# Two of the three output tiles of the second feed-forward layer by Strassen's seven products

## The chip, the core and the metric

The kernel runs on 1 core of one Trainium2 chip. The metric is the device time of one execution in microseconds (us), the median of 3 timed runs; a profile of one execution is read beside it.

## The reference

Attention with a decaying state over 4 batches, 8 heads, 768 positions of 48 values gives a matrix of 3072 tokens by 384. Two feed-forward layers follow, each 384 to 2048 to 384; the change lies in the second.

```python
x = attn_out.transpose(0, 2, 1, 3).reshape(B * S, H * D)     # 3072 x 384
h = x @ w_in;  x = (h - np.tanh(h)) @ w_out                  # layer 1
h = x @ w_in2
g = np.maximum(h, 0.0) + alpha * np.minimum(h, 0.0)          # alpha: one value per inner column
y = g @ w_out2                                               # layer 2
```

## The kernel before, in words

Every 32-bit factor of a layer's products is split into two fp32r tiles, a rounded high part (index 0) and the rest (index 1), and a product is the sum of three TensorE products: high by high, low by high, high by low (`terms`). Tokens are worked in 6 blocks j of 512 columns (`N2`), the inner 2048 columns in 16 tiles f of 128 (`KF`), the 384 columns of input and output in 3 tiles (`KC`).

One entry of `steps` is a layer, a block and an inner tile (l, j, f). A step issues, in this order of the code, which is also the order of every engine's queue:

- `mm_h` (L410): 9 products of 512 columns into one PSUM bank h; the banks 3 and 4 alternate.
- `elem_a` (L422): g from h. In layer 1 ScalarE (ACT) does the tanh, L426, and VectorE (DVE) the difference, L427. In layer 2 VectorE does both, `ga`, L429, and `gb`, L430.
- `elem_hi` (L434) on ScalarE and `elem_lo` (L438) on VectorE, issued in the next step, split gb into g, high part L436 and low part L441.
- `mm_acc1` or `mm_acc2` (L471) for the step two back (`LAG = 2`): 9 products of 512 columns, three for each of the 3 output tiles, each tile in a PSUM bank of its own. In layer 2 the blocks use the banks 0, 1, 2 and 5, 6, 7 in turn. After f = 15 each bank is copied out (L486, L484) and stored (L487).

Beside the products, in block 5 of layer 1 and block 0 of layer 2, the weights of layer 2 are turned from 64-bit words into fp32r parts by `conv_stage`: two checking passes (L108, L109), the low words (L81) and the high part (L100) on ScalarE, three operations (L94 to L96) on VectorE, the low part (L87) on GpSimd. Steps f = 6, 8 and 10 of each block of layer 2 but the last split the next block's input, `split_x2` (L495): a copy, L500, on ScalarE and a difference, L501, on GpSimd. In the attention, up to block 4 of layer 1, TensorE also has short 32-bit products: the scores `sc` (L260) and the transposes `kt` (L269). `keep_clock` and the `warm` argument of `mm_h` put idle bf16 products of 512 columns ahead of the first steps (L544, L415).

A flag computed from the inputs chooses between this program and a general one, `emit_general`, that the inputs here do not need.

Of the kernel before, what the change touches and what calls it, by code (L numbers as in the profile page):

```python
# [10 lines left out]
F32 = mybir.dt.float32  # L11
F32R = mybir.dt.float32r
# [17 lines left out]
N2 = 512  # L30
# [120 lines left out]
def emit_fast(nc, tc, qkav, w1, w2, alpha2, cst, out, x2d, c):  # L151
# [223 lines left out]
    def conv_stage(l, f, stage):  # L375
        if not 0 <= f < KF:
            return
        slot = f if l == 1 else f - EXT
        pool, tag = (wp, f"w{slot}") if slot >= 0 else (extp, f"e{f}")
        if stage == 0:  # L380
            raw_t[l, f] = conv[l].load(f, pool, tag)
        elif stage == 1:
            if l == 2:
                conv[l].check(raw_t[l, f][1], extp.tile([128, 2 * DM], BF16, tag="junk2", name="junk2"), f)
# [24 lines left out]

    terms = ((0, 0), (1, 0), (0, 1))  # L410

    def mm_h(l, f, x, n, bk, warm=0):
# [5 lines left out]
        for k, (a, b, ct) in enumerate(order):  # L418
            nc.tensor.matmul(h, w[:, a, ct * 128:(ct + 1) * 128], x[:, b, ct, :], start=(k == 0), stop=(k == 8))  # L419
# [12 lines left out]

    def elem_hi(s):
        gb, n = gb_of[s]  # L434
# [37 lines left out]
    def mm_acc2(j, f, g):  # L472
        if f == 0:
            banks = (0, 1, 2) if j % 2 == 0 else (5, 6, 7)
            acc[j] = [bank(b, [128, N2], f"o{c}") for c, b in enumerate(banks)]
        w = w_t[2, f]
        for c in range(KC):
            for i, (a, b) in enumerate(terms):
                nc.tensor.matmul(acc[j][c], w[:, a, DM + c * 128:DM + (c + 1) * 128], g[:, b, :],  # L479
                                 start=(f == 0 and i == 0), stop=(f == KF - 1 and i == 2))  # L480
            if f == KF - 1:
                e = extp.tile([128, N2], F32, tag="oe", name="oe", bufs=3)
# [4 lines left out]
                nc.sync.dma_start(out[c * 128:(c + 1) * 128, j * N2:(j + 1) * N2], e)  # L487

    x2f = {}

    def load_x2(j):
        t = extp.tile([128, KC, N2], F32, tag="x2f", name="x2f", bufs=2)
        nc.sync.dma_start(t, x2d[j])
        x2f[j] = t

# [234 lines left out]
    rechecks = {2 * KF + 4 + 2 * f: f for f in range(KF)}  # L730

    def mm_acc(s):
        l, j, f = steps[s]
        (mm_acc1 if l == 1 else mm_acc2)(j, f, g_of.pop(s))

    for s in range(F0, len(steps) + LAG):
        conv_1 = early.get(s, ())
        for f, stage in conv_1:
            if stage == 3:
                conv_stage(1, f, 3)  # L740
        if s - 1 in gb_of and s > F0:
            elem_hi(s - 1)
        if s < len(steps):
            l, j, f = steps[s]
            h = mm_h(l, f, x_t[j] if l == 1 else x_t["x2", j], N2, hb[s % 2])
            if s == u0:
                actx.close()
                extp = ctx.enter_context(tc.tile_pool(name="ext", bufs=1))
            for k, stage in conv_1:
                if stage != 3:  # L750
                    ops = conv_stage(1, k, stage)
                    if ops:
                        chains.append(ops)
            for k, stage in late.get(s, ()):
                conv_stage(2, k, stage)
            if s in rechecks:
                recheck(rechecks[s])
            if l == 1 and j == NB - 1:
# [18 lines left out]
            gb_of[s] = elem_a(l, f, h, N2), N2  # L777
            for piece in mid.get(s, ()):
                piece()
        elif s - 1 in gb_of:  # L780
            elem_lo(s - 1)
            run_chains()
        if s >= LAG + F0:
            mm_acc(s - LAG)
    ctx.close()


# [129 lines left out]
```

## Time and profile before

| what | value |
|---|---|
| median of 3 timed runs | 914.12 us (914.07 to 914.89) |
| profiled execution, its span | 913.0 us |
| TensorE busy | 899.1 us, 98% of the span |
| VectorE busy | 577.6 us, 63% |
| ScalarE busy | 367.7 us, 40% |
| GpSimd busy | 88.8 us, 10% |
| granted TensorE clock, all 40 slices | 9 tenths or more |

The span runs from the first to the last instruction of the profiled execution. Layer 2 begins near 514 us of it, its block 1 near 580 us, its last product ends near 906 us. A busy TensorE is one that always has a product in flight; how fast the products follow each other has to be read from the times of a row of equal ones. PE names TensorE's products, PEld its weight loads, DVE VectorE, ACT ScalarE, POOL GpSimd.

### The profile page before, as it was taken

What the parts mean: (1) busy time and instruction counts of PE and PEld (TensorE: products, weight loads), DVE (VectorE), ACT (ScalarE), POOL (GpSimd) and SP (SyncE); (2) the same over time, 40 slices, a digit from 0 to 9 for tenths busy, and PEclk for the clock granted to TensorE, in tenths of its full rate; (3) what the DMA queues carried; (4) which work ended last, traced back from release to release, by engine and by line L of the source; (5) the groups of instructions that cost most, each with busy time, mean ns of one, the idle gap of its engine ahead of it and who ended that gap; (6) DMA issues with size and microseconds to landing.
All of it is one profiled execution on the core that took longest, in us unless ns stands there. A gap on an engine that the chain in (4) does not pass through costs nothing.

```text
span 913.0 us, 13390 instructions
## 1 busy us (share of the span) xinstructions
PE 899.1 (98%) x5552; PEld 727.7 (80%) x5552; DVE 577.6 (63%) x835; ACT 367.7 (40%) x674; POOL 88.8 (10%) x82
## 2 busy tenths in 40 slices
PE   7899999999999999999999999999999999999997
PEld 4678887788888888788888888888888888888885
DVE  8998987766665565565466798555555555555553
ACT  2465555334545555543577665221221221221111
POOL 1110000100000000000034325010010010010000
PEclk9999999999999999999999999999999999999999
DMA  9575002124333334300364140200200100000001
GB/s 348 225 275 222 0 1 82 50 90 151 117 116 133 138 143 152 129 2 1 139 218 162 35 173 1 70 0 1 70 1 1 69 1 1 35 1 0 36 1 38
DMA packets 18212, 78.24 MB, mean 86 GB/s; under 512 B 2144, under 2 KB 2400, under 8 KB 15584
## 3 DMA queue, kind: packets, MB, share of 16 engines
q1 hardware_dynamic: 17856, 77.18, 23.0%
q8 instruction: 45, 0.74, 0.3%
q14 instruction: 23, 0.19, 0.1%
q10 hardware_dynamic: 288, 0.13, 0.1%
HBM read 67.87 MB, written 9.44 MB: 85 GB/s over the span
## 4 chain that ended last, share of the span: by engine, by line
PE 97%; DVE 2%; issue 0%; ACT 0%; POOL 0%; POOLq 0%
PE h L419 43%; PE acc L458 22%; PE o L479 21%; PE sc L260 3%; PE y L294 1%; PE idle L544 1%; PE y L307 1%; PE U L324 1%; PE y L298 1%; PE kt L269 1%; DVE iA L231 1%; DVE P L281 1%; PE y L302 0%; DVE A L220 0%; DVE x L339 0%
## 5 line engine op out<-in xcount | busy, mean ns | idle before, releaser
L419 PE MATMUL h<-x,w 128*128 128x512 f32 x1728 | 423.5, 390 | 0.6 <-ACT w L100 0.5
L419 PEld LDWEIGHTS h<-x,w 128*128 128x128 f32 x1728 | 324.4, 188 | 68.9 <-ACT w L100 1.0
L436 ACT CAST g<-gb 128x512 fp32r<-128x512 f32 x192 | 119.1, 620 | 349.0 <-DVE gb L430 272.5
L458 PE MATMUL acc<-g,w 128*128 128x512 f32 x864 | 216.5, 395 | 0.0
L479 PE MATMUL o<-g,w 128*128 128x512 f32 x864 | 211.2, 389 | 0.0
L441 DVE TENSOR_TENSOR g<-gb,g 128x512 fp32r<-128x512 f32 x192 | 135.8, 707 | 101.7 <-ACT g L436 101.5
L479 PEld LDWEIGHTS o<-g,w 128*128 128x128 f32 x864 | 162.2, 188 | 33.5
L458 PEld LDWEIGHTS acc<-g,w 128*128 128x128 f32 x864 | 159.5, 188 | 35.5 <-issue 0.8
L427 DVE TENSOR_TENSOR gb<-h,ga 128x512 f32<-128x512 f32 x96 | 66.1, 689 | 115.5 <-ACT ga L426 115.5
L429 DVE TENSOR_SCALAR ga<-h,al 128x512 f32<-128x512 f32 x96 | 72.0, 749 | 85.9 <-PE h L419 85.9
L426 ACT ACTIVATE ga<-h 128x512 f32<-128x512 f32 x96 | 56.5, 589 | 90.0 <-PE h L419 89.9
L430 DVE SCALAR_TENSOR_TENSOR gb<-h,ga 128x512 f32<-128x512 f32 x96 | 66.4, 691 | 3.3
L221 POOL TENSOR_TENSOR qkav_t<-qkav_t,A 128x512 f32<-128x512 f32 x20 | 24.6, 1232 | 367.0 <-DVE ac L222 324.8
L501 POOL TENSOR_TENSOR x<-x2f,x 128x512 fp32r<-128x512 f32 x18 | 24.4, 1355 | 237.0 <-ACT x L500 235.1
L87 POOL TENSOR_TENSOR w<-cv,w 128x384 fp32r<-128x384 f32 x32 | 35.5, 1128 | 103.9 <-DVE g L441 51.6
L100 ACT CAST w<-cv 128x768 fp32r<-128x768 f32 x32 | 26.7, 835 | 28.0 <-DVE cv L96 28.0
L231 DVE TENSOR_TENSOR_SCAN iA<-qkav_t,d1s 128x516 f32<-128x516 f32 x20 | 36.2, 1808 | 0.7
L95 DVE SCALAR_TENSOR_TENSOR cv<-raw,cv 128x768 uint32<-128x768 uint32 x32 | 35.2, 1101 | 0.1
L281 DVE TENSOR_TENSOR P<-sc,mask 128x512 f32<-128x512 f32 x48 | 30.8, 682 | 1.1 <-PE sc L260 0.7
L96 DVE CUSTOM_DVE_ANT_0 cv<-raw,cv 128x1536 uint16<-128x1536 uint16 x32 | 30.5, 952 | 0.6
L243 ACT ACTIVATE junk<-qkav_t,lim 128x512 bf16<-128x512 f32 x40 | 29.0, 724 | 0.7
L81 ACT ACTIVATE raw<-raw 128x768 uint32<-128x768 uint32 x32 | 28.9, 902 | 0.0
(84 smaller groups left out, 483.1 us busy)
## 6 DMA issues: line engine op xcount, KB each, us to landing
raw<-w SPq DMA_DIRECT2D x48, 768.0 KB, 6.4
qkav_t<-qkav SPq DMA_DIRECT2D x20, 1028.0 KB, 5.0
x2d<-x2e SPq DMA_DIRECT2D x18, 256.0 KB, 2.2
x2f<-x2d SPq DMA_DIRECT2D x6, 768.0 KB, 5.7
out<-oe SPq DMA_DIRECT2D x18, 256.0 KB, 2.1
qv<-qkav SPq DMA_DIRECT2D x8, 256.0 KB, 6.8
ak<-qkav SPq DMA_DIRECT2D x3, 516.0 KB, 7.0
ak<-qkav SPq DMA_DIRECT2D x1, 260.0 KB, 3.6
```

The lines of the kernel that those rows point to most:

```text
L87: self.nc.gpsimd.tensor_tensor(w[:, 1, i:i + DM], t.bitcast(F32)[:, i:i + DM], w[:, 0, i:i + DM].bitcast(F32), op=ALU.subtract)
L231: lambda: nc.vector.tensor_tensor_scan(iA[:, AW - 1:0:-1], a[:, AW - 1:0:-1], d1s[:, AW - 1:0:-1], 1.0, op0=ALU.mult, op1=ALU.add),
L281: nc.vector.tensor_tensor(P, scs[u], mask[:, None, :].to_broadcast([128, 4, CH]), op=ALU.mult)
L419: nc.tensor.matmul(h, w[:, a, ct * 128:(ct + 1) * 128], x[:, b, ct, :], start=(k == 0), stop=(k == 8))
L426: nc.scalar.activation(ga, h, ACTF.Tanh)
L427: nc.vector.tensor_tensor(gb, h, ga, op=ALU.subtract)
L429: nc.vector.tensor_scalar(ga, h, 0.0, al2[:, f:f + 1], op0=ALU.min, op1=ALU.mult)
L430: nc.vector.scalar_tensor_tensor(gb, h, 0.0, ga, op0=ALU.max, op1=ALU.add)
L436: nc.scalar.copy(g[:, 0], gb)
L441: chains.append([lambda: nc.vector.tensor_tensor(g[:, 1], gb, g[:, 0].bitcast(F32), op=ALU.subtract)])
L458: nc.tensor.matmul(acc[j][c], w[:, a, DM + c * 128:DM + (c + 1) * 128], g[:, b, :], start=(first and i == 0), stop=(last and i == 2))
L479: nc.tensor.matmul(acc[j][c], w[:, a, DM + c * 128:DM + (c + 1) * 128], g[:, b, :], start=(f == 0 and i == 0), stop=(f == KF - 1 and i == 2))
```

## The change

From f = 8 of block 1 of layer 2 to f = 13 of block 5, the steps are taken in pairs (35 of them): two inner tiles, two of the three output tiles and the two halves of the 512 columns make a 2 by 2 by 2 product of blocks. Its eight block products, each of 256 columns and three terms, are replaced by Strassen's seven. The third output tile (`c2`) and h keep their products of 512 columns. `mm_mixed` issues behind most of these one product of 256 columns from `queue` (10 in the even step of a pair, 11 in the odd one). The first pair skips three places, so that from then on the queue runs three products behind. f = 0 to 7 of block 1 and f = 14, 15 of block 5 keep the plain form (`mm_plain`); the last two are issued after the last step.

The sums of the data (`ta`, `tb`) are made for each pair by `elem_pair` on VectorE and split into high and low parts by both engines; the sums of the weights are made once, by `sums_w`, in steps f = 0 to 8 of block 1. `close_1` and `close_2` add the seven products of a block up when it ends; they, and the copy of the third tile, `store_o2`, are put in `post` and issued inside `elem_pair`. In layer 2 the first of the two operations of `elem_a` goes from VectorE to ScalarE, as a Relu with scale -alpha, with one more input test (`alpha_signs`: alpha must not be negative). `oe`, `junk2` and `x2e` now share three buffers, `x2f` has one buffer in place of two.

```diff
 def elem_a(l, f, h, n):
...
-            nc.vector.tensor_scalar(ga, h, 0.0, al2[:, f:f + 1], op0=ALU.min, op1=ALU.mult)
-            nc.vector.scalar_tensor_tensor(gb, h, 0.0, ga, op0=ALU.max, op1=ALU.add)
+            nc.scalar.activation(ga, h, ACTF.Relu, scale=c["nal"][:, f:f + 1])
+            nc.vector.scalar_tensor_tensor(gb, h, 0.0, ga, op0=ALU.max, op1=ALU.subtract)
...
+    def sums_w(p, stage):
...
+                v.tensor_tensor(whole[:, 2 * i:2 * i + 2].rearrange("p a b -> p (a b)"), hi, lo, op=ALU.add)
+            a11, a21, a12, a22 = (whole[:, i] for i in range(4))
+            v.tensor_tensor(t[:, 0], a21, a22, op=ALU.add)
+            v.tensor_tensor(t[:, 3], a11, a21, op=ALU.subtract)
+            v.tensor_tensor(t[:, 1], t[:, 0], a11, op=ALU.subtract)
+            v.tensor_tensor(t[:, 2], a12, t[:, 1], op=ALU.subtract)
...
+            nc.scalar.copy(s_t[p][:, 0], t[:, 0:3])
+            nc.scalar.copy(s_t[p, 3][0], t[:, 3])
+            t = s_t.pop((p, "t"))
+            v.tensor_tensor(s_t[p][:, 1], t[:, 0:3], s_t[p][:, 0].bitcast(F32), op=ALU.subtract)
+            v.tensor_tensor(s_t[p, 3][1], t[:, 3], s_t[p, 3][0].bitcast(F32), op=ALU.subtract)
...
+    def elem_pair(s, gb):
...
+        if s % 2 == 0:
+            if not plain(s):
+                ta = cvp.tile([128, 2, HN], F32, tag="cv", name="ta")
+                v.tensor_tensor(ta[:, 0], right, left, op=ALU.subtract)
+                t_of[q] = gb, ta
+            nc.scalar.copy(g[:, 0], gb)
+            run_post()
+            pair_lo(q - 1, 1)
+            low()
+            return
+        nc.scalar.copy(g[:, 0], gb)
...
+        v.tensor_tensor(ta[:, 1], right, b0[:, HN:N2], op=ALU.subtract)
+        v.tensor_tensor(tb[:, 0], b0[:, 0:HN], ta[:, 1], op=ALU.add)
+        run_post()
+        low()
+        v.tensor_tensor(tb[:, 1], left, tb[:, 0], op=ALU.subtract)
+        gs = [extp.tile([128, 2, 2, HN], F32R, tag=n, name="g") for n in ("gta", "gtb")]
+        nc.scalar.copy(gs[0][:, 0], ta)
+        nc.scalar.copy(gs[1][:, 0], tb)
+        t_of[q] = ta, tb, gs
+        pair_lo(q, 0)
...
+        ops = products(x["P1"], lambda a: w_out(f0, 0, a), lambda b: g0[:, b, 0:HN], first, False)
+        ops += products(x["P2"], lambda a: w_out(f1, 0, a), lambda b: g1[:, b, 0:HN], opens, False)
+        ops += products(x["P3"], lambda a: sw[:, a, 2], lambda b: g1[:, b, HN:N2], False, last)
+        ops += products(x["P5"], lambda a: sw[:, a, 0], lambda b: ga[:, b, 0], False, end)
+        ops += products(x["P7"], lambda a: s3[a], lambda b: ga[:, b, 1], first, False)
+        ops += products(x["P6"], lambda a: sw[:, a, 1], lambda b: gb[:, b, 0], False, end)
...
+        ops += products(x["P4"], lambda a: w_out(f1, 1, a), lambda b: gb[:, b, 1], opens, last)
...
+    def close_1(j):
...
+        nc.scalar.copy(e0[:, 0:HN], x["P1"])
+        v.tensor_tensor(u2, e0[:, 0:HN], x["P6"], op=ALU.add)
+        v.tensor_tensor(e1[:, 0:HN], u2, x["P7"], op=ALU.add)
+        v.tensor_tensor(e0[:, HN:N2], u2, x["P5"], op=ALU.add)
+        v.tensor_tensor(e1[:, HN:N2], e1[:, 0:HN], x["P5"], op=ALU.add)
+        x["e", 0], x["e", 1] = e0, e1
+        if j < NB - 1:
+            v.tensor_tensor(e0, e0, x["1"], op=ALU.add)
...
+    def mm_mixed(s, order):
...
+        wide = order + products(fast[j]["c2"], lambda a: w_out(f, 2, a), lambda b: g_of[t][:, b],
+                                f == 0, f == KF - 1)
+        skip = 3 if plain(t - 1) else 0
+        for i, op in enumerate(wide):
+            op()
+            if skip <= i < 10 + f % 2:
+                pop()
+        if f == KF - 1:
+            post.append(lambda: store_o2(j))
```

How the order of the instructions moves is shown at three places.

TensorE in the middle of layer 2, before: a step is nine products into h, then three for each output tile.

```order
L419 MATMUL h<-x,w 128x512 x9
L479 MATMUL o_5933<-g,w 128x512 x3
L479 MATMUL o_5934<-g,w 128x512 x3
L479 MATMUL o_5935<-g,w 128x512 x3
```

TensorE in the change, at the end of block 2 and the start of block 3 (o_6132, o_6133: P6 and P4 of block 2; o_6134: its third tile; o_6743: P1 of block 3, o_6744: P2 and P3 of block 3; ws: a weight sum).

```order
L603 MATMUL o_6132<-g,ws 128x256
L603 MATMUL o_6134<-g,w 128x512
L419 MATMUL h<-x,w 128x512
L603 MATMUL o_6133<-g,w 128x256
...
L603 MATMUL o_6743<-g,w 128x256
...
L603 MATMUL o_6744<-g,w 128x256
L603 MATMUL o_6747<-g,w 128x512
L603 MATMUL o_6744<-g,ws 128x256
L603 MATMUL o_6747<-g,w 128x512 x2
```

Products of 512 and 256 columns alternate, and the third product into o_6744, which reads the low part of the odd step's g, stands right behind the ninth product into h of the next step.

VectorE in the change at the same place, from `elem_a` of the odd step f = 1 of block 3 on (u and oe: the closing sums of block 2).

```order
L437 SCALAR_TENSOR_TENSOR gb<-h,ga 128x512
L583 TENSOR_TENSOR ta<-gb 128x256
L584 TENSOR_TENSOR tb<-gb,ta 128x256
L684 TENSOR_TENSOR u_6724<-oe,o_6132 128x256
L685 TENSOR_TENSOR oe<-u_6724,o_6132 128x256
L686 TENSOR_TENSOR oe<-u_6724,o_6130 128x256
L687 TENSOR_TENSOR oe<-oe,o_6130 128x256
L690 TENSOR_TENSOR oe<-oe,o_6131 128x512
L560 TENSOR_TENSOR g<-gb,g 128x512
```

Five closing sums now stand between gb and the low part of g (L560); in the pairs inside a block only ta and tb stand there.

ScalarE in the change in block 0 of layer 2, one step with a weight check, a high part and an input split (before, the row L436 ACTIVATE was not there, and VectorE read h itself).

```order
L449 CAST g<-gb 128x512
L100 CAST w<-cv 128x768
L108 ACTIVATE junk_5120,sums<-raw 128x768
L109 ACTIVATE junk_5120,out_of<-junk_5120,lim 128x768
L81 ACTIVATE raw<-raw 128x768
L738 CAST x<-x2f 128x512
L436 ACTIVATE ga<-h,nal 128x512
```

The reading of h is now the last of seven operations of ScalarE's step.

## Rows read from the trace of the kernel before

**Rows 1.** The page: busy time by engine, and the chain that ended last.

```profile
PE 899.1 (98%) x5552; PEld 727.7 (80%) x5552; DVE 577.6 (63%) x835; ACT 367.7 (40%) x674; POOL 88.8 (10%) x82
...
PE 97%; DVE 2%; issue 0%; ACT 0%; POOL 0%; POOLq 0%
```

**Rows 2.** Busy time by stretch: us, each engine's busy us (x instructions), clock, DMA.

```profile
540.00:560.00 20.00, 20.00 (x90) 16.57 (x89) 18.14 (x22) 13.37 (x24) 10.20 (x9) 1.00 0.00 0
...
613.00:678.00 65.00, 65.00 (x288) 53.84 (x288) 33.88 (x49) 13.16 (x22) 3.88 (x3) 1.00 0.07 25
```

**Rows 3.** Timeline of one step of layer 2: start us, us, engine, what.

```profile
699.42 2.00 PEld L479 LDWEIGHTS o<-g,w 128*128 128x128 f32 x9
699.64 2.20 PE L479 MATMUL o<-g,w 128*128 128x512 f32 x9
699.85 0.75 DVE L429 TENSOR_SCALAR ga<-h,al 128x512 f32<-128x512 f32 x1 [1.15 <-PE h L419]
700.63 0.69 DVE L430 SCALAR_TENSOR_TENSOR gb<-h,ga 128x512 f32<-128x512 f32 x1
701.43 0.62 ACT L436 CAST g<-gb 128x512 fp32r<-128x512 f32 x1 [3.46 <-DVE gb L430]
...
701.68 2.20 PE L419 MATMUL h<-x,w 128*128 128x512 f32 x9
702.09 0.69 DVE L441 TENSOR_TENSOR g<-gb,g 128x512 fp32r<-128x512 f32 x1 [0.76 <-ACT g L436]
```

**Rows 4.** Timelines of TensorE: the last 27 products, and idle bf16 products.

```profile
899.92 6.28 PE L479 MATMUL o<-g,w 128*128 128x512 f32 x27
...
29.18 1.90 PE L415 MATMUL h<-idle_w 128*128 128x512 bf16 x8
```

**Rows 5.** Timeline of the weight loads of the scores of one tile.

```profile
264.87 0.97 PEld L260 LDWEIGHTS sc<-qkav_t 64*128 64x128 f32 x16 [0.17 <-issue]
```

**Rows 6.** Groups by line and shape: busy us, mean ns of one, idle before.

```profile
L419 PE MATMUL h<-x,w 128*128 128x512 f32 x1728 | 423.5, 390 | 0.6 <-ACT w L100 0.5 <-DVE w L104 0.2
L419 PEld LDWEIGHTS h<-x,w 128*128 128x128 f32 x1728 | 324.4, 188 | 68.9 <-ACT w L100 1.0 <-DVE w L104 0.6
L458 PE MATMUL acc<-g,w 128*128 128x512 f32 x864 | 216.5, 395 | 0.0
L479 PE MATMUL o<-g,w 128*128 128x512 f32 x864 | 211.2, 389 | 0.0
L436 ACT CAST g<-gb 128x512 fp32r<-128x512 f32 x192 | 119.1, 620 | 349.0 <-DVE gb L430 272.5 <-DVE gb L427 73.0 <-DVE sums L358 3.5
L426 ACT ACTIVATE ga<-h 128x512 f32<-128x512 f32 x96 | 56.5, 589 | 90.0 <-PE h L419 89.9
L260 PEld LDWEIGHTS sc<-qkav_t 64*128 64x128 f32 x320 | 19.4, 187 | 4.9 <-issue 4.9
L352 DVE TENSOR_TENSOR S<-U,S 128x256 f32<-128x256 f32 x16 | 6.6, 415 | 0.0
```

**Rows 7.** Timeline of VectorE, two operations of which neither needs the other.

```profile
266.37 1.28 DVE L281 TENSOR_TENSOR P<-sc,mask 128x512 f32<-128x512 f32 x2
```

**Rows 8.** Timeline of block 0 of layer 2, weights being converted.

```profile
544.15 0.62 PE L419 MATMUL h<-x,w 128*128 128x512 f32 x2
...
546.05 0.63 ACT L436 CAST g<-gb 128x512 fp32r<-128x512 f32 x1 [3.75 <-DVE gb L430]
546.58 0.83 ACT L100 CAST w<-cv 128x768 fp32r<-128x768 f32 x1
547.31 0.91 ACT L108 ACTIVATE junk<-raw 128x768 bf16<-128x768 f32 x1
548.22 0.74 DVE L429 TENSOR_SCALAR ga<-h,al 128x512 f32<-128x512 f32 x1
548.35 0.94 ACT L109 ACTIVATE junk<-junk,lim 128x768 bf16<-128x768 bf16 x1
549.28 0.89 ACT L81 ACTIVATE raw<-raw 128x768 uint32<-128x768 uint32 x1
550.08 0.61 ACT L500 CAST x<-x2f 128x512 fp32r<-128x512 f32 x1
550.59 0.62 ACT L436 CAST g<-gb 128x512 fp32r<-128x512 f32 x1
```

More of the change, by code (lines that the diff above doesn't have):

```diff
@@ new lines, in pair_lo, with products @@
+    def pair_lo(q, i):
+        if q in t_of:
+            t, g = t_of[q][i], t_of[q][2][i]
+            nc.vector.tensor_tensor(g[:, 1], t, g[:, 0].bitcast(F32), op=ALU.subtract)
+    def products(out, w, g, start, stop, cut=False):
+        ops = []
+        for i, (a, b) in enumerate(terms):
+            for n in (slice(0, HN), slice(HN, N2)) if cut and i == 0 else (slice(None),):
+                ops.append(lambda a=a, b=b, i=i, n=n: nc.tensor.matmul(
+                    out[:, n], w(a), g(b)[:, n], start=(start and i == 0), stop=(stop and i == 2)))
+        return ops
@@ new lines, in fast_open, with store_o2 @@
+    def fast_open(j):
+        b3, b1, b4, b2, free = spare
+        x = fast[j] = {n: bank(b, [128, N2], f"o{n}") for n, b in zip("3142", (b3, b1, b4, b2))}
+        x["c2"] = bank(0, [128, N2], "o2")
+        spare[:] = [free, b4, b1, b2, b3]
+        x["P1"], x["P5"] = x["3"][:, 0:HN], x["3"][:, HN:N2]
+        x["P2"], x["P3"] = x["1"][:, 0:HN], x["1"][:, HN:N2]
+        x["P7"], x["P6"] = x["4"][:, HN:N2], x["4"][:, 0:HN]
+        x["P4"] = x["2"][:, 0:HN]
+        return x
+    def store_o2(j):
+        e = sp.tile([128, N2], F32, tag="x2e", name="oe")
+        nc.scalar.copy(e, fast[j]["c2"])
+        nc.sync.dma_start(out[256:384, j * N2:(j + 1) * N2], e)
@@ new lines, in mm_plain @@
+    def mm_plain(j, s, cs=range(KC)):
+        f = steps[s][2]
+        x = fast[j] if j in fast else fast_open(j)
+        last = f == KF - 1
+        for c in cs:
+            o = x["12"[c]] if c < 2 else x["c2"]
+            seen = f > 0
+            for op in products(o, lambda a: w_out(f, c, a), lambda b: g_of[s][:, b], not seen, last,
+                               c == 1 and j == NB - 1 and f == KF - 2):
+                op()
+            if last:
+                if c == 2:
+                    store_o2(j)
+                else:
+                    nc.vector.tensor_tensor(x["e", c], o, x["e", c], op=ALU.add)
+                    nc.sync.dma_start(out[c * W:(c + 1) * W, j * N2:(j + 1) * N2], x["e", c])
@@ new lines, in queue_pair @@
+    def queue_pair(j, s):
+        f0, f1 = steps[s][2], steps[s][2] + 1
+        x = fast[j] if j in fast else fast_open(j)
+        first = f0 == (KF // 2 if j == 1 else 0)
+        last = f1 == KF - 1
+        end = last or (j == NB - 1 and f1 == KF - 3)
+        opens = first and j != 1
+        g0, g1 = g_of[s], g_of[s + 1]
+        ga, gb = t_of[s // 2][2]
+        sw, s3 = s_t[f0 // 2], s_t[f0 // 2, 3]
+        ops = products(x["P1"], lambda a: w_out(f0, 0, a), lambda b: g0[:, b, 0:HN], first, False)
[4 more added lines that the diff above has]
+        ops += products(x["P6"], lambda a: sw[:, a, 1], lambda b: gb[:, b, 0], False, end)
+        if end:
+            ops[-1] = (ops[-1], lambda: close_1(j))
+        ops += products(x["P4"], lambda a: w_out(f1, 1, a), lambda b: gb[:, b, 1], opens, last)
+        if last:
+            ops[-1] = (ops[-1], lambda: close_2(j))
+        queue.extend(ops)
@@ new lines, in pop @@
+    def pop():
+        if queue:
+            op = queue.pop(0)
+            if isinstance(op, tuple):
+                op, after = op
+                post.append(after)
+            op()
+    def close_1(j):
+        v = nc.vector
+        x = fast[j]
+        e0, e1 = (sp.tile([128, N2], F32, tag="x2e", name="oe") for _ in range(2))
+        u2 = gp.tile([128, HN], F32, tag="ga", name="u2")
+        nc.scalar.copy(e0[:, 0:HN], x["P1"])
[6 more added lines that the diff above has]
+            v.tensor_tensor(e0, e0, x["1"], op=ALU.add)
+            nc.sync.dma_start(out[0:W, j * N2:(j + 1) * N2], e0)
@@ new lines, in close_2 @@
+    def close_2(j):
+        x = fast[j]
+        e1 = x["e", 1]
+        n = slice(0, N2 if mixed(j) else HN)
+        nc.vector.tensor_tensor(e1[:, n], e1[:, n], x["2"][:, n], op=ALU.add)
+        nc.sync.dma_start(out[W:2 * W, j * N2:(j + 1) * N2], e1)
+    def mm_mixed(s, order):
+        t = s - LAG
+        j, f = steps[t][1:]
+        if f % 2 == 0:
+            queue_pair(j, t)
+        wide = order + products(fast[j]["c2"], lambda a: w_out(f, 2, a), lambda b: g_of[t][:, b],
+                                f == 0, f == KF - 1)
+        skip = 3 if plain(t - 1) else 0
+        for i, op in enumerate(wide):
+            op()
+            if skip <= i < 10 + f % 2:
+                pop()
+        if f == KF - 1:
+            post.append(lambda: store_o2(j))
@@ L489, in emit_fast, with finish_fast @@
+    def finish_fast():
+        while queue:
+            pop()
+        s = len(steps) - 2
+        for c in range(KC):
+            mm_plain(NB - 1, s, (c,))
+        for c in range(KC):
+            mm_plain(NB - 1, s + 1, (c,))
     x2f = {}
     def load_x2(j):
-        t = extp.tile([128, KC, N2], F32, tag="x2f", name="x2f", bufs=2)
+        t = kp.tile([128, KC, N2], F32, tag="part", name="x2f")
         nc.sync.dma_start(t, x2d[j])
@@ L730, in emit_fast @@
     rechecks = {2 * KF + 4 + 2 * f: f for f in range(KF)}
+    l2 = NB * KF
+    w_sums = {}
+    for p in range(KF // 2):
+        for stage in range(2):
+            w_sums.setdefault(l2 + KF + p + stage, []).append((p, stage))
     def mm_acc(s):
         l, j, f = steps[s]
-        (mm_acc1 if l == 1 else mm_acc2)(j, f, g_of.pop(s))
+        if l == 2 and j > 0:
+            if plain(s) and s < len(steps) - 2:
+                mm_plain(j, s)
+        else:
+            (mm_acc1 if l == 1 else mm_acc2)(j, f, g_of.pop(s))
     for s in range(F0, len(steps) + LAG):
@@ L757, in emit_fast @@
                 recheck(rechecks[s])
+            if s == 3 * KF:
+                alpha_signs()
             if l == 1 and j == NB - 1:
@@ L776, in emit_fast @@
             run_chains()
-            gb_of[s] = elem_a(l, f, h, N2), N2
+            gb = elem_a(l, f, h, N2)
+            if l == 2 and j > 0:
+                elem_pair(s, gb)
+            else:
+                gb_of[s] = gb, N2
             for piece in mid.get(s, ()):
                 piece()
+            for p, stage in w_sums.get(s, ()):
+                sums_w(p, stage)
         elif s - 1 in gb_of:
```

73 lines of the change are left out of this document (65 added, 8 removed).

## The prediction

> **What bounds the kernel now.** I read the page first: TensorE is busy for 98% of the span and has 97% of the chain that ended last, and the other engines have no 3% of it [rows 1]. The table by stretch says that this holds in layer 2 too: in 65 us of it VectorE works 33.9 us and ScalarE 13.2, at a granted clock of 1.00 (the 2.4 GHz level) [rows 2]. The timeline of a step shows why nothing waits: nine products take their 2.04 us (from 699.64 to 701.68), g is ready within 3.2 us of h's end, and its reader comes a step later [rows 3]. So layer 2 costs what its products cost. The last 27 give the price of one: (6.28 - 0.39) / 26 = 0.2265 us for 512 columns [rows 4, 6]. Fewer or narrower products are the only gain there is, and a wait put in front of a product is a loss in full. About 0.2%, 1.8 us, is what can be told from no change here.
>
> **Term A, the products.** A pair of steps had 2 tiles x 2 steps x 3 terms = 12 products of 512 columns, 12 x 226.5 = 2718 ns. It gets 7 x 3 = 21 of 256 columns; h and the third tile stay. All depends on the price p of a product of 256 columns between two of 512, which no row has. Below, p is bounded by the weight loads: each product has its own, 188 ns long [rows 6]. Loads of 187 ns for the scores start every (0.97 - 0.19) / 7 = 111 ns, so a load need not be waited out, but 111 is the least that a row shows (with half the height) [rows 5, 6]. Half of 226.5 is 113.3. If what an fp32r product costs beyond a bf16 one, (1.90 - 0.38) / 7 = 217 ns [rows 4], comes per product and not per column, p = 217 / 2 + 9.5 = 118. I take 113.3, between these and nearest to the scores' row: 21 x 113.3 = 2379, 339 ns less a pair, 35 pairs: **-11.9 us** (-13.5 at 111, -8.4 at 118).
>
> The Trainium skill (TensorE: Matmul & The Clock Gate, Back-to-back issue gap) gives N / 2.4 + 2.5 ns at the full clock: 215.8 for 512 columns and, as an estimate, 109.2 for 256. The row's 226.5 is 10.7 over it, so the measurement decides; with 109.2 this term would be -14.9 us and the sum 907.8.
>
> **Term B, the ends of the blocks.** Inside a block the odd step's g must come within one step, no longer two. Call h's end 0. Relu (as the tanh, 589 ns) ends at 0.63, gb (691) at 1.36 [rows 3, 6]. ta and tb are 256 columns wide, 415 ns each as the nearest row, and depend on each other: 1.82 and 2.27 [rows 6]. ScalarE's high part ends near 2.1, the low part (690 ns) at 2.9 to 3.0. Its reader is the eighth place behind: 4 wide and 3 narrow products end the step, 9 and 8 follow, so 13 x 226.5 + 11 x 113.3 ns less the 0.39 us that h's last product takes to end: 3.80. Spare: 0.8 us, no wait. The other sums have more room: VectorE's whole work for a pair is some 5.9 us of the pair's 7.8.
>
> At four block ends (1 to 2 up to 4 to 5) `close_1` stands before the low part. Its P1 copy on ScalarE comes behind the high part and ends near 2.35; then 0.42 us for u2 (2.39 to 2.81), e1 from 2.84, two sums that need each other no more (start to start 0.34), the 512-wide one from 3.85; back-to-back independent operations of 0.68 start 0.60 apart [rows 7]. The low part runs from 4.46 to 5.15: TensorE waits 5.2 - 3.8 = 1.4 us, four times: **+5.7 us**. In block 5 the close comes before f = 15's low part, without ta, tb and the 512-wide sum: ready at 4.55 against 15 wide and 6 narrow products, 3.69, **+0.9 us**. Bounds: with half of the closing operations' 2.1 us hidden each wait is 0.4 us, with none of them overlapping it is 1.9.
>
> **Term C, Relu in ScalarE's queue.** In block 0 before, VectorE read h, already 3.45 us after h's end (544.77 to 548.22) [rows 8]; the next use of that bank is 27 products after its last one, 6.1 us, less the drain and the 1.4 us of both readings: 4.3 us of room. Now Relu stands behind ScalarE's step of high part, L100, L108, L109, L81 and L500, 546.05 to 550.59 [rows 8], 4.5 us, plus Relu and gb with their hand-overs, 1.4: 5.9 us of chain in a step of 4.08. Steps f = 6 and 8 are so, f = 10 nearly; the step between is light and catches up. With the room nearly spent, each may put up to 1.9 us on TensorE, or nothing: VectorE loses 0.75 us a step there, and in layer 1 the tanh stood in the same place behind the same work with 0.5 us of TensorE's idle time in the whole program [rows 6]. Between 0 and 4 I take half: **+2.0 us**.
>
> **At nothing.** The weight sums, some 2 us of VectorE a step in f = 0 to 8 of block 1, lie beside 1.3 us of gb and low part in a step of 4.08; if VectorE fell behind there, g would still have its two steps. The single `x2f` buffer: the next load is issued when GpSimd has split the last, and is used six steps later. The stores stay off the path, and behind the last product stand one copy and one store as before.
>
> **The sum.** -11.9 + 5.7 + 0.9 + 2.0 = -3.3 us on the profiled span of 913.0; the median stands 1.1 above that span, and the difference is put on it: 914.1 - 3.3 = **910.8 us**.
>
> **The rivals.** *The surplus is per product* (p = 118): A is -8.4, the sum +0.2 us, 914.3: no change. For it: bf16 products of the same width are 9.5 ns shorter, so some of the price is no price of columns. Against: the scores' loads keep 111 ns.
>
> *Products of mixed kinds disturb each other* (slower). Place: every pair of a wide and a narrow product. Products into `acc` of layer 1, where the attention's products come between, last 395 ns against 389 of `o` [rows 6]. If the wide and the narrow one each pay these 6 ns, a narrow one costs in effect 113.3 + 12 = 125: A is -3.3, the sum +5.3, **919.4 us**. It decides from 120 ns on, where A is -6.9 and the sum +1.7. Of the same kind and worse: a wide product must wait for its whole load (188 ns), which no longer has a wide one to hide behind; at p = 130 nothing of A is left, 922.7. The loads of the scores speak against that one.
>
> The Trainium skill (Perfetto Trace Analysis, Optimizing Tensor Performance, Matmuls) says that larger matmuls are more efficient than smaller ones; by that rule the direction would be this rival's, and no row of the trace has an fp32r product of 256 columns that could settle it.
>
> *The waits are not there* (faster): VectorE closes a block in time and block 0 hides Relu as layer 1 hid the tanh. B is 0.4 x 4 + 0.3, C nothing: 914.1 - 10.0 = 904.1.
>
> *The change does not do what it says*: the new test of alpha sends the inputs to the general program. The reference draws alpha from 0 up, so I give it no chance.
>
> **How the numbers follow.** My forecast, with p from 111 to 117: 0.50. Per product: 0.20. Mixed kinds or an exposed load: 0.20. No waits: 0.10. The forecast's own bounds are 907.2 (p = 111, C nothing) to 915.6 (p = 117, C = 4); the other cases reach from 904.1 to 922.7 and beyond. The range 905 to 920 leaves out the ends of these, some 0.15. Faster by over 0.2% (under 912.3): 0.42 of the forecast's 0.50 and the last rival, 0.52; within: the rest of the forecast and most of the second case, 0.23; slower (over 915.9): 0.25.
>
> **What would show it.** A: in the middle of block 3 a step, from h's first product to the next one's, lasts 12 x 0.2265 + 10.5 x 0.1133 = 3.91 us against 4.08; products of 256 start their successors 113 ns on, those of 512 226. B: TensorE idle for 1.4 us behind h's last product in f = 2 of blocks 2 to 5, released by VectorE's low part, and 0.9 us near the end. C: idle time before h in block 0, released by VectorE's gb. VectorE's busy time rises by some 70 us (35 pairs x 3.1, the sums and closes 36, less 96 x 0.75), ScalarE's by some 110 (96 Relu, 70 copies). It is wrong if the step is over 4.0 us, or if idle time of TensorE stands inside the blocks.

## The result, and the profile after

| | before | after |
|---|---|---|
| median | 914.32 us (914.07 to 914.89, 4 runs) | 919.40 us (919.12 to 920.61, 4 runs) |
| span of the profiled execution | 913.0 us | 917.5 us |

The ratio is 1.0058, 95% interval 1.0043 to 1.0072: **slower by 5 us**, where 3.3 us less were forecast.

The page of the changed kernel: busy time, the chain that ended last, and three groups by line.

```profile
PE 896.5 (98%) x5862; PEld 734.5 (80%) x5868; DVE 628.7 (69%) x1043; ACT 471.7 (51%) x854; POOL 87.9 (10%) x82
...
PE 85%; DVE 8%; ACT 4%; issue 1%; POOL 0%; ACTq 0%; DVEq 0%; POOLq 0%
...
L603 PE MATMUL o<-g,w 128*128 128x256 f32 (+1 forms) x616 | 177.4, 337 | 5.5 <-DVE g L560 4.1
L603 PE MATMUL o<-g,ws 128*128 128x256 f32 x420 | 116.9, 278 | 0.0
L436 ACT ACTIVATE ga<-h,nal 128x512 f32<-128x512 f32 x96 | 65.9, 686 | 70.2 <-PE h L419 68.5
```

TensorE's busy share is the same 98% as in [rows 1], but its part of the chain fell from 97% to 85%: VectorE and ScalarE now have 12% of it. The waits of TensorE in layer 2 (us in total, times, longest) name the places:

```profile
PE o L603 <- DVE g L560: 4.1, 5, 0.8
PE h L419 <- DVE gb L437: 1.2, 2, 0.9
PE o L603 <- ACT g L576: 1.0, 1, 1.0
```

That is 6.3 us of waiting, so the products themselves can have saved little. From start to start the loss is larger than these records say, as they put a product's end some 0.16 us behind the earliest start of the next (0.39 us against 0.23 for a wide one). The table by stretch answers to [rows 2]:

```profile
613.00:678.00 65.00, 63.04 (x344) 53.72 (x344) 48.29 (x94) 32.09 (x55) 3.93 (x3) 1.00 0.07 25
678.00:743.00 65.00, 64.06 (x358) 55.28 (x358) 45.08 (x86) 31.50 (x54) 3.90 (x3) 1.00 0.07 25
```

Each such 65 us holds one block's end. TensorE is idle for 0.9 us in the second stretch and for 2.0 in the first, which has one wait more; the granted clock stays at 1.00 (2.4 GHz). VectorE is busy for 45 and 48 of 65 us only, so at the ends of the blocks TensorE waits for a chain and not for a full engine. In the first half of block 1 that is otherwise, as shown below.

How the products follow each other is read from TensorE's timeline near the end (every second row is a product of 256 columns):

```profile
894.65 0.39 PE L419 MATMUL h<-x,w 128*128 128x512 f32 x1
894.88 0.28 PE L603 MATMUL o<-g,ws 128*128 128x256 f32 x1
895.00 0.39 PE L419 MATMUL h<-x,w 128*128 128x512 f32 x1
895.23 0.28 PE L603 MATMUL o<-g,ws 128*128 128x256 f32 x1
...
896.38 0.39 PE L603 MATMUL o<-g,w 128*128 128x512 f32 x1
```

From 894.65 to 896.38 there are five pairs of a wide and a narrow product, (896.38 - 894.65) / 5 = 346 ns each. Less the 226.7 ns of a wide one (4.08 / 18 before), a narrow one costs some **120 ns** (eighteen in a row in e1 below: 2.16 / 18 = 120.0), and 113.3 was taken. 120.0 is 256 / 2.4 + 13.3, and 226.7 is 512 / 2.4 + 13.3: it looks as if every product paid 13.3 ns beside its columns. This is theory 1 of the experiments.

To see where in layer 2 the time goes, the start of `gb` on VectorE in every step was compared with that of the same step before (us later than before, called the lag; e3 and so on are the experiments below):

```
start of gb     after  e3     e6     e2     e4     e8
block 1 f = 0   1.57   0.09   2.41   2.47   1.71  -0.75
block 1 f = 13  3.36   1.95   2.73   2.64   3.51  -1.36
block 2 f = 1   3.06   1.65   2.44   2.32   3.22  -1.67
block 2 f = 3   4.31   2.90   3.68   3.10   3.49  -1.37
block 3 f = 1   3.32   1.96   2.69   1.04   2.72  -2.96
block 3 f = 3   4.56   3.21   3.94   1.56   2.73  -2.91
block 4 f = 3   4.82   3.48   4.19   0.28   1.84  -4.19
block 5 f = 3   5.07   3.76   4.44  -1.00   0.92  -5.47
block 5 f = 15  4.32   3.01   3.70  -2.68   0.23  -6.67
```

In the changed kernel the lag grows in block 0, grows again in the first half of block 1, jumps by 1.25 at every block's end (f = 1 to 3), and falls between the ends by about 0.15 us a pair of steps (4.45 at f = 5 of block 3, 3.86 at f = 13: four pairs). Profiled executions differ at the start of layer 2 already (TensorE's first product into h starts 0.70 us later than before in e2, 0.21 earlier in the change, 0.69 earlier in e8), so only changes within one column count. The lag is VectorE's: TensorE's own first products into h fall behind by 1.8 us in block 0 (from -0.21 us to 1.57), not at all from there to f = 10 of block 1, and by 1.0 us (1.58 to 2.57) between f = 10 and 11. Up to there g has two steps until it is read, and they hide VectorE's lag. Then comes this wait, for the g of f = 9, the odd step of the first pair and the first that has one step only:

```profile
619.32 0.40 PE L419 MATMUL h<-x,w 128*128 128x512 f32 x1
620.74 0.39 PE L603 MATMUL o<-g,w 128*128 128x256 f32 x1 [1.02 <-ACT g L576]
```

The end of block 2, from the end of h of the odd step on (ScalarE, VectorE, and TensorE's products around the wait):

```profile
715.47 0.69 ACT L436 ACTIVATE ga<-h,nal 128x512 f32<-128x512 f32 x1 [1.86 <-PE h L419]
...
716.19 0.69 DVE L437 SCALAR_TENSOR_TENSOR gb<-h,ga 128x512 f32<-128x512 f32 x1 [1.58 <-ACT ga L436]
...
717.84 0.42 DVE L684 TENSOR_TENSOR u<-oe,o 128x256 f32<-128x256 f32 x1
...
719.29 0.68 DVE L690 TENSOR_TENSOR oe<-oe,o 128x512 f32<-128x512 f32 x1
...
719.40 0.39 PE L419 MATMUL h<-x,w 128*128 128x512 f32 x1
...
719.89 0.68 DVE L560 TENSOR_TENSOR g<-gb,g 128x512 fp32r<-128x512 f32 x1
...
720.63 0.61 PE L603 MATMUL o<-g,w 128*128 128x256 f32 x2 [0.83 <-DVE g L560]
```

The closing sums stand from 717.84 to 719.89 between `tb` and the low part of g; TensorE's product that reads it should have followed 0.23 us after 719.40 and starts at 720.63, 1.0 us late. Another 0.27 us is lost at 718.6, before an earlier product of the same step; the two make the jump of 1.25.

Block 1, f = 6, ScalarE, VectorE and GpSimd:

```profile
599.66 0.76 DVE L532 TENSOR_TENSOR whole<-w 128x256 f32<-128x256 f32 x2
...
601.39 0.68 DVE L437 SCALAR_TENSOR_TENSOR gb<-h,ga 128x512 f32<-128x512 f32 x1
602.10 0.62 ACT L576 CAST g<-gb 128x512 fp32r<-128x512 f32 x1 [1.93 <-DVE gb L437]
...
602.76 0.69 DVE L560 TENSOR_TENSOR g<-gb,g 128x512 fp32r<-128x512 f32 x1 [0.69 <-ACT g L576]
...
603.94 1.34 POOL L739 TENSOR_TENSOR x<-x2f,x 128x512 fp32r<-128x512 f32 x1 [34.05 <-ACT x L738]
604.04 1.52 DVE L532 TENSOR_TENSOR whole<-w 128x256 f32<-128x256 f32 x1
```

VectorE has no gap in these steps but the 0.69 us in which it waits for ScalarE's high part, and its step is 4.38 us long, 0.30 over TensorE's 4.08. Where GpSimd's split runs beside it, an addition that takes 0.42 us elsewhere takes 1.52. This happens twice, at f = 6 and f = 8, so that of the 4.27 us by which `gb` falls behind from f = 1 to f = 8 (1.57 to 5.84), 2.1 come from seven steps of 0.30 and 2.2 from these two additions.

### The profile page after: what moved, and what is told of

It reads as the page before. It is cut to its first block, busy times and chain, and to the rows that moved or that the text cites. A ratio compares the mean times of both kernels' runs of the same rounds, so it can differ in the third digit from the quotient of the medians.

```text
span 917.5 us, 14543 instructions
## 1 busy us (share of the span) xinstructions
PE 896.5 (98%) x5862; PEld 734.5 (80%) x5868; DVE 628.7 (69%) x1043; ACT 471.7 (51%) x854; POOL 87.9 (10%) x82
## 4 chain that ended last, share of the span: by engine, by line
PE 85%; DVE 8%; ACT 4%; issue 1%; POOL 0%; ACTq 0%; DVEq 0%; POOLq 0%
PE h L419 38%; PE acc L471 22%; PE o L603 14%; PE sc L261 3%; DVE gb L437 2%; PE o L492 2%; PE y L295 1%; PE y L308 1%; PE idle L782 1%; PE U L325 1%; PE y L299 1%; DVE g L560 1%; ACT ga L436 1%; PE kt L270 1%; DVE whole L532 1%
## 5 line engine op out<-in xcount | busy, mean ns | idle before, releaser
L419 PE MATMUL h<-x,w 128*128 128x512 f32 x1728 | 492.3, 391 | 1.8 <-DVE gb L437 1.2
L603 PE MATMUL o<-g,w 128*128 128x256 f32 (+1 forms) x616 | 177.4, 337 | 5.5 <-DVE g L560 4.1
L603 PEld LDWEIGHTS o<-g,w 128*128 128x128 f32 x616 | 112.5, 188 | 21.1 <-DVE g L560 6.0
L603 PE MATMUL o<-g,ws 128*128 128x256 f32 x420 | 116.9, 278 | 0.0
L454 DVE TENSOR_TENSOR g<-gb,g 128x512 fp32r<-128x512 f32 x112 | 78.2, 699 | 34.7 <-ACT g L449 34.5
L436 ACT ACTIVATE ga<-h,nal 128x512 f32<-128x512 f32 x96 | 65.9, 686 | 70.2 <-PE h L419 68.5
L603 PEld LDWEIGHTS o<-g,ws 128*128 128x128 f32 x420 | 79.1, 188 | 1.6
L560 DVE TENSOR_TENSOR g<-gb,g 128x512 fp32r<-128x512 f32 x80 | 54.7, 684 | 5.8 <-ACT g L571 3.0
L590 ACT CAST g<-tb 128x512 fp32r<-128x512 f32 x35 | 21.7, 621 | 33.2 <-DVE tb L587 33.2
```

Of the source, the lines that this page charges most:

```text
L419: ops = [lambda k=k, a=a, b=b, ct=ct: nc.tensor.matmul(h, w[:, a, ct * 128:(ct + 1) * 128], x[:, b, ct, :], start=(k == 0), stop=(k == 8)) ...
L436: nc.scalar.activation(ga, h, ACTF.Relu, scale=c["nal"][:, f:f + 1])
L454: chains.append([lambda: nc.vector.tensor_tensor(g[:, 1], gb, g[:, 0].bitcast(F32), op=ALU.subtract)])
L560: v.tensor_tensor(g[:, 1], gb, g[:, 0].bitcast(F32), op=ALU.subtract)
L603: ops.append(lambda a=a, b=b, i=i, n=n: nc.tensor.matmul(out[:, n], w(a), g(b)[:, n], start=(start and i == 0), stop=(stop and i == 2)))
```

## The experiments

**Theory**: (1) a product pays 13.3 ns whatever its width and neighbours, so the narrow ones save 0.2 us a pair at most; (2) the closing sums cost TensorE 1.2 to 1.6 us at each block's end; (3) VectorE is the bound of the first half of block 1 through the weight sums; (4) the Relu costs 1.6 us in block 0. **Rival**: narrow products are cheap (113 ns) and only suffer between wide ones, so that the order is at fault.

**e1, widths of the products, in the kernel before.** The cut does not show the part in `mm_h` that puts the products of blocks 2 and 3 between those into h.

```diff
+    def acc2_ops(j, f, g):
...
+            parts = {3: 2, 4: 2}.get(j, 4 if j == 5 and c == 0 else 1)
...
+                for p in range(parts):
+                    n = slice(p * N2 // parts, (p + 1) * N2 // parts)
```

> The kernel before, with only the products into the three output tiles of layer 2 changed in shape or order; the arithmetic is the same. Block 2: the 512-column products into h and into the output tiles alternate. Block 3: every output product is cut in two of 256 columns, and two of these stand behind each product into h. Block 4: the same cut, but all nine products into h first, then the 18 narrow ones. Block 5: the three products into the first output tile are cut in four of 128 columns. Theory 1 (an fp32r product costs its columns at the full clock plus 13.3 ns, whatever its width and its neighbours): 226.7, 120.0 and 66.7 ns a product, so a step lasts 4.08 us in block 2, 4.20 in blocks 3 and 4 (9 x 226.7 + 18 x 120) and 4.20 in block 5 (15 x 226.7 + 12 x 66.7); in all some 48 x 0.12 = 5.8 us more than before. Rival (the price goes by columns, and products of mixed kinds disturb each other by some 6 ns each): 4.19 us in block 2, over 4.20 in block 3, 4.08 in blocks 4 and 5. Rival (a weight load has to be waited out from one narrow product to the next, 111 to 188 ns): 4.04 us or more in block 4 and at least 15 x 226.7 + 12 x 111 = 4.73 us in block 5.

Measured: 929.96 us (one run; 914.44 before). A step of block 4 (nine wide products, then eighteen narrow) and one of block 5 in TensorE's timeline (the rows `o` of block 5 count twelve of 128 columns and six of 512 together):

```profile
797.80 2.23 PE L419 MATMUL h<-x,w 128*128 128x512 f32 x9
799.86 2.31 PE L485 MATMUL o<-g,w 128*128 128x256 f32 x18
802.02 0.86 PE L419 MATMUL h<-x,w 128*128 128x512 f32 x3
```

```profile
874.80 2.90 PE L485 MATMUL o<-g,w 128*128 128x128 f32 x18
877.54 2.22 PE L419 MATMUL h<-x,w 128*128 128x512 f32 x9
879.60 2.67 PE L485 MATMUL o<-g,w 128*128 128x128 f32 x17
```

A step of block 4 lasts 802.02 - 797.80 = 4.22 us. By the starts of `gb`, block 2 stays at 4.08 and block 3 has 4.20. So 512-column products of two kinds may alternate for nothing, and two narrow ones cost 13 ns more than one wide one in either order, as theory 1 has it (4.20) and not the price by columns. In block 5, though, a step lasts 879.60 - 874.80 = 4.80 us, near the last rival's 4.73: less 15 wide ones, the twelve of 128 columns take 1.40, 117 ns each and not 66.7. Below some width, a product costs a constant. Taken one by one in that timeline, products of 128 columns start 109 to 116 ns apart, 112 in the mean; the rest of the 117 falls on the wide products behind them, of which the second to the tenth take 232 ns each and the others 227. A floor of 112 ns can't make the 120 of a 256-column product, and half of 226.7 is 113.3: so neither the floor nor a price by columns alone explains the 120, and a part per product does. Behind 18 narrow ones the nine wide ones of block 4 take 799.86 - 797.80 = 2.06 us, where nine took 2.04 before. The whole run's 15.5 us are these: 16 x (0.12 + 0.14 + 0.72).

**e5, other widths, between wide products** (in block 2 the two parts of a product stand together behind a wide one).

```diff
+    cuts = {2: [(0, 320, 512)] * 3, 3: [(0, 128, 256, 384, 512)] + [(0, 512)] * 2,
+            4: [(0, 256, 512)] * 2 + [(0, 512)]}
...
```

> The kernel before, with only the products into the output tiles of layer 2 cut otherwise; the arithmetic is the same. Block 2: each cut in 320 and 192 columns, both behind a product into h. Block 3: the three into the first tile cut in four of 128 columns, each of the twelve between two of 512. Block 4: the six into the first two tiles cut in two of 256, each of the twelve between two of 512, as in the change but without its VectorE and ScalarE work. Theory 1 (columns plus 13.3 ns for every product): 146.7, 93.3, 66.7 and 120.0 ns, so a step lasts 4.20 us in block 2 (9 x 13.3 ns more than 4.08), 4.20 in block 3 and 4.16 in block 4. Theory 1b (columns plus 13.3 ns, but never under the 113 ns that the products of 128 columns took back to back, even between two wide ones): 4.38 us in block 2 (9 x (226.7 + 146.7 + 113)), 4.76 in block 3 (15 x 226.7 + 12 x 113), 4.16 in block 4. Rival (mixed kinds disturb each other by 6 ns each, price by columns): 4.08 plus some 0.1 in all three.

Measured: 933.38 us (one run; 914.79 before). Two steps each of blocks 2, 3 and 4, by VectorE's timeline, and the products of block 3 in TensorE's:

```profile
662.24 0.69 DVE L432 SCALAR_TENSOR_TENSOR gb<-h,ga 128x512 f32<-128x512 f32 x1
...
666.68 0.69 DVE L432 SCALAR_TENSOR_TENSOR gb<-h,ga 128x512 f32<-128x512 f32 x1
...
747.13 0.69 DVE L432 SCALAR_TENSOR_TENSOR gb<-h,ga 128x512 f32<-128x512 f32 x1
...
751.92 0.69 DVE L432 SCALAR_TENSOR_TENSOR gb<-h,ga 128x512 f32<-128x512 f32 x1
...
816.82 0.69 DVE L432 SCALAR_TENSOR_TENSOR gb<-h,ga 128x512 f32<-128x512 f32 x1
...
821.06 0.69 DVE L432 SCALAR_TENSOR_TENSOR gb<-h,ga 128x512 f32<-128x512 f32 x1
```

```profile
744.78 0.22 PE L488 MATMUL o<-g,w 128*128 128x128 f32 x1
744.84 0.44 PE L419 MATMUL h<-x,w 128*128 128x512 f32 x1
745.12 0.22 PE L488 MATMUL o<-g,w 128*128 128x128 f32 x1
745.18 0.44 PE L419 MATMUL h<-x,w 128*128 128x512 f32 x1
```

Steps of 4.44, 4.79 and 4.24 us. In block 3 a pair takes 340 ns: the narrow product's successor starts 60 ns behind it, but the wide one then lasts 280. So 128 columns cost some 115 ns between wide products too, and the wide neighbour hides nothing of it: theory 1b (4.76), not theory 1 (4.20). Block 2 is also nearer to 1b (4.38). Block 4 is 0.08 over both: there a pair costs 4.24 / 12 = 353 ns, some 7 more than in the change's rows above. That is of the rival's size; in the changed kernel itself it averages 3 ns (below). The change has both kinds itself (six pairs from 750.07 to 752.19 at 353 ns, those just before at 347). What makes the difference between these pairs was not tried.

The Trainium skill (TensorE: Matmul & The Clock Gate, Back-to-back issue gap) says that in a stream of load and product the spacing is set by both, and that the formula without a load counts too little for narrow products. The 115 to 117 ns for 128 columns agree with the rule, though not with its figure, 81 ns; its 131 ns for 512 columns is not seen either (226.7).

**e2, the order alone**: the narrow products behind the wide ones of the step.

```diff
-        for i, op in enumerate(wide):
+        for op in wide:
             op()
-            if skip <= i < 10 + f % 2:
-                pop()
+        for _ in range(10 + f % 2 - skip):
+            pop()
```

> The change, but each step's 10 or 11 narrow products stand behind all 12 wide ones of the step in place of one behind each. Theory 1 (13.3 ns a product whatever stands beside it): the narrow ones still start their successors 120 ns on, and the step's products cost as much as in the change. What the order does change is where the low parts of g are read: the product that waited at the ends of the blocks now stands behind 12 wide ones, so the five waits go (four of 1.6 us by the trace, and one of 0.9 us): 919.4 - 7 = some 912.5 us. Rival (mixed kinds disturb each other): the narrow products fall to 113 ns, 35 x 21 x 6.7 ns = 4.9 us are gained on top, some 907.5 us, and a step inside block 3 falls from 3.99 to 3.91 us.

Measured: **911.61 us** (5 runs; before 914.44), ratio 0.9966, interval 0.9952 to 0.9980. That is 0.9% under the change and beats the kernel before. A step's products in TensorE's timeline, and TensorE's waits in layer 2:

```profile
728.93 0.84 PE L603 MATMUL o<-g,w 128*128 128x512 f32 x3
729.61 1.48 PE L603 MATMUL o<-g,ws 128*128 128x256 f32 x11
730.92 2.23 PE L419 MATMUL h<-x,w 128*128 128x512 f32 x9
```

```profile
PE h L419 <- DVE gb L437: 1.2, 2, 0.9
PE o L603 <- DVE g L560: 0.4, 1, 0.4
```

Eleven narrow products take 730.92 - 729.61 = 1.31 us, 119 ns each: back to back they cost what they cost between wide ones. From f = 3 of a block to f = 3 of the next, e2 gains 1.28 us, 0.16 a pair of steps (the change: 0.15), so the rival's 113 ns falls. What went are the five waits at the ends, 4.1 us in all: the reader of the low part of g now stands behind the step's twelve wide products. The 0.4 us that stays is not at an end but in block 1 (at 622.52), behind the weight sums, where the change lost 1.0.

**e3, the Relu of block 0 back on VectorE.**

```diff
+            if j == 0:
+                nc.vector.tensor_scalar(ga, h, 0.0, al2[:, f:f + 1], op0=ALU.min, op1=ALU.mult)
+                nc.vector.scalar_tensor_tensor(gb, h, 0.0, ga, op0=ALU.max, op1=ALU.add)
...
```

> The change, but in block 0 of layer 2 VectorE makes both operations of g as before; from block 1 on ScalarE does the Relu. Theory: the Relu stands last in ScalarE's queue beside the weight conversion and costs what the starts of the steps of block 0 have fallen behind, 1.6 us: 917.8 us, and no idle time of TensorE before a product into h of block 0. Rival (it costs nothing there and the lag comes from the loads or from GpSimd): 919.4 us, and block 0 falls behind as in the change.

Measured: 917.41 us (6 runs), ratio 1.0032, 1.0020 to 1.0044, so some 2 us of the 5 are gone. TensorE's first products into h keep their place through block 0 (0.15 us behind at f = 0 and at f = 15), where they lost 1.8 us in the change, and TensorE no longer waits for `gb`. The theory holds; the rival falls.

**e4, the closing sums behind the low part**, from copies that ScalarE makes.

```diff
+        nc.scalar.copy(e1, x["4"])
+        nc.scalar.copy(e0, x["3"])
...
+        ends_1.append(rest)
```

> The change, but at a block's end ScalarE copies both banks that hold P1, P5, P6 and P7, and VectorE makes the closing sums from the copies after the low part of g and tb in place of before them. Theory: the sums in front of the low part are what TensorE waits for at the ends of the blocks, four times 1.6 us and once 0.9; they go, some 912.5 us, and no idle time of TensorE is left that ends with the low part of g. Rival (the wait comes from the place of the reader in TensorE's order, or from the banks that the next block needs, and is given back there): 918 to 920 us.

Measured: 914.69 us (11 runs; before 914.44), ratio 1.0004, 0.9995 to 1.0013. All waits for the low part of g are gone; TensorE keeps these two:

```profile
PE h L419 <- DVE gb L437: 1.2, 2, 0.9
PE o L608 <- ACT g L577: 1.0, 1, 1.0
```

The theory holds in kind; its 7 us were too many, as 4.9 came (1.0058 less 1.0004). In the table the jump from f = 1 to f = 3 is 0.27 us at the first end and 0.01 at the next, in place of 1.25, so the edit takes 1.0 to 1.25 us off an end, and 1.6 was expected.

**e6, the weight sums spread out.**

```diff
-    for p in range(KF // 2):
+    for k, p in enumerate((4, 5, 6, 7, 0, 1, 2, 3)):
...
-            w_sums.setdefault(l2 + KF + p + stage, []).append((p, stage))
+            w_sums.setdefault(l2 + (14, 15, 16, 18, 19, 20, 21, 23)[k] + stage, []).append((p, stage))
```

> The change, but the weight sums are made from the last steps of block 0 on (steps 14 to 16, 18 to 21 and 23 of layer 2, pairs of the second half of f first) in place of f = 0 to 8 of block 1, so that no two lie in every step and GpSimd's splits meet fewer of them. Theory (VectorE was the bound of f = 0 to 9 of block 1, where the starts of the steps fell behind by 2.1 us): most of these 2.1 us go, some 917.3 us, and the steps of block 1 last 4.08 us in place of 4.38. Rival (VectorE's load moves to where it is as scarce, or the lag comes from TensorE): 919.4 us, with the steps of 4.38 us at another place.

Measured: 917.92 us (6 runs; before 914.79), ratio 1.0033, 1.0021 to 1.0046. From f = 0 to f = 13 of block 1 the lag grows by 0.3 us, not by 1.8, so the sums cost 1.5 us where they stood in the change. (Not all of the 1.8 is loss: in both kernels h ends 1.0 us later once narrow products stand between its own, from f = 11 on, and the first pairs give some of it back.) The wait for ScalarE's g is gone. Steps over 4.08 us remain where two sums still follow each other. Two additions beside GpSimd's splits still take 1.5 us each here (604.29 and 611.73), and no wait follows, so they alone are not the cause of it. Whether the row of steps that are too long would have made the wait without them was not tried.

**e7, e2 with e3 and e6; e8, these with e4.**

> The change with three edits together: narrow products behind the step's wide ones, the Relu of block 0 back on VectorE, the weight sums spread out. Theory (the losses are separate places and add): 911.6 of the first edit alone, less 2.0 (Relu, as measured) and less 2.1 (sums): some 907.5 us, about 0.7% under the kernel before. Rival (one hides another, as where VectorE catches up anyway): 909.5 to 911.6 us.

> The same with the closing sums made after the low part too, from ScalarE's copies. Theory (with the narrow products last in the step the ends of the blocks have no wait left but 0.4 us in all): 0 to 0.4 us less than with the three edits. Rival (the wait at the ends is still there and hidden in the steps behind): up to 2 us less.

Measured: e7 908.99 us, ratio 0.9939 (0.9926 to 0.9953), and e8 **908.36 us, ratio 0.9932** (0.9918 to 0.9945), each 5 runs against 914.79. The three losses are separate places and nearly add: 907.5 was expected on 914.4, which is 908 on the 914.8 of these runs. The 1.0 us that e7 is short of it lies near the uncertainty, and the traces have a reason for it: with e2's order the wait behind the weight sums was 0.4 us already and not 1.0, so that e6 had less to give back. The fourth edit, worth 4.9 us alone, gives 0.6 more here, within the uncertainty: e2 had removed the same wait. The page of e8, its busy time and chain:

```profile
PE 891.9 (98%) x5862; PEld 736.3 (81%) x5868; DVE 641.4 (71%) x1059; ACT 463.4 (51%) x843; POOL 88.9 (10%) x82
...
PE 96%; DVE 3%; DMA 0%; issue 0%; ACT 0%; DVEq 0%
```

TensorE has its part of the chain back (96%), with VectorE busier than in the change. In e7 and e8 TensorE has no wait left in layer 2, and both beat the change and the kernel before.

## Why the prediction was wrong

*Term A, the products, -11.9 us*: the step that failed. Its p = 113.3, half a wide product, was taken as nearest to the scores' loads. Between block ends a pair of steps gains 0.14 to 0.15 us, so 8.16 - 0.145 = 8.015 us stand for 24 wide products (h and the third tile) and 21 narrow ones: p = (8.015 - 24 x 0.2267) / 21 = 122.6 ns, 120 of it the price alone and some 3 for what the wide ones beside them take longer (in e1 the nine behind narrow ones took 2.06 us, not 2.04). The term is 35 x -0.145 = **-5.1 us**. The bf16 product of the same width [rows 4] had shown a part that is not columns, 9.5 ns; the text gave it to a rival as 118 and set against it the scores. Their 111 ns are what lies between the starts of two pairs of half-height loads, each for a product of 128 columns, and such products cost 112 ns in e1 too: that is the floor of narrow products and no price by columns.

By the formula of the Trainium skill (TensorE: Matmul & The Clock Gate, Back-to-back issue gap), 109.2 ns was the estimate; the traces disagree (120 ns). The rule of the Trainium skill that larger matmuls are more efficient (Perfetto Trace Analysis, Optimizing Tensor Performance, Matmuls) agrees with the traces: 0.44 ns a column at 512, 0.47 at 256, 0.9 at 128.

*Term B, the ends, +5.7 and +0.9*: right. The place, the releaser and the five waits are as foretold (four times the 1.4 of the text is 5.6, not 5.7). An end costs 1.25 us of jump plus the 0.14 that a pair would have gained, 1.4 as forecast, four times 5.6, though 0.27 us of it comes at another product than foretold. The last wait is 0.73 us of idle time:

```profile
909.08 1.89 PE L603 MATMUL o<-g,w 128*128 128x512 f32 x7 [0.73 <-DVE g L560]
```

The product before it starts at 907.96, so this start is 909.08 - 907.96 - 0.23 = 0.9 us late.

*Term C, the Relu, +2.0*: right; 1.8 us by TensorE's products (from -0.21 to 1.57 within block 0, nothing in e3), some 2 by the medians. That it came out at the half of 0 to 4 was a guess and not a reading. Two waits before h, both released by VectorE's gb, make it:

```profile
542.79 2.34 PE L419 MATMUL h<-x,w 128*128 128x512 f32 x9 [0.27 <-DVE gb L437]
552.17 2.11 PE L419 MATMUL h<-x,w 128*128 128x512 f32 x8 [0.92 <-DVE gb L437]
```

*"At nothing", the weight sums*: the second step that failed. From 598.99 to 601.39 they take 2.4 us of a step, not 2.0, and the 0.69 us in which VectorE waits for the high part cannot be filled in program order: 0.69 + 0.69 + 0.6 + 2.4 = 4.38. That g has two steps of slack helps against one late step, not against a row of steps that are all too long; and the wait came where g has one step only, as Term B itself says of an odd step: the product at 620.74 reads the g of f = 9, and its h had ended at 615.7. It cost some **1.5 us** (1.79 us of lag from f = 0 to 13 of block 1 in the change, 0.32 in e6; the medians, which are less sure, say 2.3). Part of it may be due to the two additions beside GpSimd, 2.2 us of VectorE's time that the prediction did not have either. The rest of "at nothing" held: no wait for `x2f` or a store shows.

The sum with what was measured: -5.1 + 5.6 + 0.9 + 1.8 + 1.5 = +4.7 us; the spans differ by 4.5, the medians by 5.1. Of the 8.4 us between the forecast of -3.3 and the 5.1 that came, 6.8 are the price of the narrow products and 1.5 the weight sums.

*The rivals.* "The surplus is per product" was right in its mechanism and 2 ns low in its size. "Mixed kinds disturb" gave 919.4, the time that came, by another sum: its p = 125 came from 12 ns of disturbance where 3 were found, and its sum had no price for the weight sums. "The waits are not there" falls. Of the marks set in advance, three failed: the step is 4.01 us long and not 3.91; TensorE is idle inside a block (1.0 us at f = 10 of block 1); and VectorE's busy time rose by 51 us (577.6 to 628.7), not by 70. ScalarE's rose by 104, and some 110 were forecast.

## What to carry to other kernels

Price a narrower product by its own width and not by a share of the wide one: saving an eighth of the arithmetic by halving the width gave 35 x (12 x 226.7 - 21 x 120) = 7 us at most, of which 5 were left, and each wait that the extra sums bring must be set against that. Where a product reads what a slow chain makes, put those that don't need it in front: the same products in another order were worth 0.9%. An engine that is lightly used on average still sets the pace where its step, waits in program order included, is longer than that of the bound engine; add up the step, not the busy share.

## What the chip showed beside this

- An fp32r product took 226.7 ns at 512 columns and 120 at 256, but 112 at 128 back to back, 115 to 117 with what it adds to the wide ones behind or beside it. The first two fit the columns at 2.4 GHz plus 13.3 ns; the last is a floor. That the weight load makes it is likely (each product has its own) but was not tried apart from the product.
- Wide products are slower behind narrow ones: in e1 232 ns each for the second to the tenth behind twelve of 128 columns, and 227 after that. In e5 the successor of a wide one starts 280 ns on where a product of 128 columns stands before it.
- An addition of VectorE on 256 columns took 1.52 us beside a subtraction of GpSimd, and two of them 0.76 without it.
- ScalarE's Relu with a scale per partition took 686 ns, the tanh of the same size 589 [rows 6].
